# One order of work in a fused state-space and dense kernel: the second dense layer's third product before its second, and one weight load moved

## The chip, the cores and the metric

The kernel runs on one core of a Trainium2 chip. The metric is the device time of one execution in microseconds (us). Before the change it is 587.95 us, the median of 3 runs (587.34 to 588.11). The execution that was profiled took 587.96 us, with a span of 586.7 us between its first and its last instruction. TensorE's granted clock is 1.0 throughout.

## The reference

```python
def _A_ref(x, ...):                       # S5: a diagonal complex state space
    Lam_bar = jnp.exp(dt * Lam)
    B_bar = ((Lam_bar - 1.0) / Lam)[:, None] * Bmat
    Bu = jnp.einsum("bld,pd->blp", x + 0j, B_bar)
    for t in range(L):
        h = Lam_bar[None, :] * h + Bu[:, t, :]
    y = 2.0 * jnp.einsum("blp,dp->bld", hseq, Cmat).real + x * Dskip

def _B_ref(x, w1, b1, w2):                # two dense layers with Mish between
    h = jnp.einsum("bsd,df->bsf", x, w1) + b1
    sp = jnp.log1p(jnp.exp(-jnp.abs(h))) + jnp.where(h > 0, h, 0)
    return jnp.einsum("bsf,fd->bsd", h * jnp.tanh(sp), w2)

xn = _layernorm(x)
out = x + _A_ref(xn, ...) + _B_ref(xn, B_w1, B_b1, B_w2)
```

There are 2048 tokens of width 1024, the state has 1024 complex entries, and the dense layers are 1024 to 3584 to 1024 wide. All inputs are bfloat16.

## The kernel before

**Blocks.** The tokens are worked off in four blocks of 512. A block has dense 1 (28 tiles of 128 hidden columns, with Mish), the state space's projection in, its scans and its projection out, and dense 2, all of which TensorE feeds into eight banks of PSUM. The third block, and the fourth, compute dense 1, the projection in and dense 2 by a scheme of the Strassen kind: the two operands are halved in both dimensions, and seven products of halves stand in for eight. Products 1, 2 and 4 multiply raw halves of the activations, products 5, 6, 7 and 3 sums of them; on the side of the weights products 1, 2 and 3 use raw halves, the others sums.

**Dense 2 of the third block.** Twenty of the 28 activation tiles take part in the seven products, ten in either half (`NFG[2]` is 5, so there are five units of two tiles in each product); the other eight (`PLAIN`) are multiplied in the usual way. A product has two halves i, for two tiles of 128 tokens, each with its own bank and ten matmuls. Product 1 writes banks 0 and 2, product 2 banks 4 and 6, product 7 banks 1 and 3, product 5 banks 5 and 7.

**The ring.** Weights reach TensorE through `ring`, seven slots of 512 KB in SBUF. `items` is the list of everything that goes through it, in order; item number n goes into slot n modulo 7. In the third block an item is a pair of units of 256 KB: `ws` are two units of w1, `tp` two units of w2 as the kernel has prepared them (raw or sums) in the DRAM tensor `w2d`; unit 7p+g belongs to the p-th product of `KIND = (1, 7, 2, 5, 6, 3, 4)` and the group g. So units 0 to 4 are product 1's, 7 to 11 product 7's, 14 to 18 product 2's, 21 to 25 product 5's. `w2` items are raw tiles for the plain part, `c` items the projection out. The loads are issued by SyncE's queue (SP), one after the other (`ring_load`, L481 for `tp`, L486 for `ws`), and each waits until TensorE has done with what was in the slot's half, and for a `tp` unit until its store to `w2d` has landed. Both units of a pair count on one semaphore, and a reader waits for both. Items are released in their order only: `release` moves on while the next item in the list has been used up, and `ring_fill` then issues up to seven items from there.

**The stores.** POOL's queue stores the units to `w2d` (`d2_store`, L1269): the raw ones (products 1, 2, 3) of a group when `d2_row` has scaled it, the sums (5, 7, 6, 4) as VectorE makes them in `d2_sums` (L1297), one at each `k0` of the order. The first three of either kind share a semaphore, which counts only when all three have landed.

**The order by hand.** The instructions of the third block follow a string, `STEPS`; each engine works off its own instructions in that order. The tokens that matter here:

| token | what | engine |
|---|---|---|
| x1 ... y4, z7, z4 | a product of dense 1 for the quads x, y, z of four tiles: 8 matmuls (L1063) | TensorE |
| ez4, ey4, ... | its evacuation (L1083, L1086, L1100) | ACT, VectorE |
| D11, D10 | product 1 of dense 2, halves 1 and 0: 10 matmuls each (L1544); D20, D21, D70, D71 likewise for products 2 and 7 | TensorE |
| X5, X6, X3, X4 | a whole product, 20 matmuls | TensorE |
| g2, g6, g7 | Mish of tiles 12-19, 20-23, 24-27 (L931) | ACT |
| G7 ... G13 | scaling of two tiles each, Gn of tiles 2n and 2n+1 (L938) | ACT |
| t0, t1, t2, ta0 | the sums of activations for products 7, 5, 6 and 3 (L1399) | VectorE |
| E3; lr0, li0; ns, tr | the next block's layer norm | VectorE; ACT, VectorE; ACT, SP |
| r3 to r7; sc, to, so; al | rotations, scans, rotations back; scaling | VectorE; ACT |
| kp2, kp3; kp0, kp1 | product 1's (kp2), 6's (kp3), 7's (kp0), 5's (kp1) banks set aside in `KS` (L1624; L1618) | ACT; VectorE |
| pl24, pl10, pl12, pl26 | two plain tiles each, into all eight banks: 16 matmuls | TensorE |
| Y, Q, fin | the projection out, its end, the addition to x (L1679) | TensorE, TensorE, VectorE |

Product 2 reads tiles 14 to 23 of the activations (their second halves of tokens), the ones that G7 to G11 scale; its matmuls take them in that order, two from each G. t1 reads both the tiles 0 to 9 and 14 to 23 and stands behind G10. Every reader and writer of a buffer waits as program order has it: an instruction that overwrites a tile waits for the earlier ones that read it. A matmul's reading is told by the next matmul of TensorE that signals, which for these halves is the last of the ten.

The pair lists are made at the end of the part that builds `items` (L441 and on): `W_ITEMS[blk]` is the list of w1 pairs in the order of their use in `STEPS` or `LAST`; for the third block it has 19 items, the last of which is the single unit of z4. `SPLIT` is the third and the fourth block, `NB - 1` the fourth.

Of the kernel before, what the change touches and what calls it, by code (L numbers as in the profile page):

```python
# [142 lines left out]
def bass_parallel_sum__ssm_conv_s5__dense_activation_mish__prompt_kernel(  # L143
    nc: bass.Bass,
    A_x: bass.AP,
    A_Lambda_re: bass.AP,
    A_Lambda_im: bass.AP,
    A_B_re: bass.AP,
    A_B_im: bass.AP,
    A_C_re: bass.AP,  # L150
    A_C_im: bass.AP,
    A_log_dt: bass.AP,
    A_Dskip: bass.AP,
    B_x: bass.AP,
    B_w1: bass.AP,
    B_b1: bass.AP,
    B_w2: bass.AP,
    out: bass.AP,
):
    build_kernel(nc, A_x, A_Lambda_re, A_Lambda_im, A_B_re, A_B_im, A_C_re, A_C_im,  # L160
                 A_log_dt, A_Dskip, B_w1, B_b1, B_w2, out)


def build_kernel(nc, A_x, A_Lambda_re, A_Lambda_im, A_B_re, A_B_im, A_C_re, A_C_im,
# [10 lines left out]
    NF = F // P  # L175
# [5 lines left out]
    FAST = 1  # L181
    NPL = 12
    SPLIT = range(2, NB)
    GROUPS = ((0, 7), (7, NPL), (NPL, NPL + 8), (NPL + 8, NF), (12, 16), (16, 20), (20, 24), (24, 28))
    TILES = [*range(12)]
    NFG = {2: 5, 3: GF}
    W2_ORDER = (*range(10), 12, 10, 11, 13)
    EARLY, LATE = ((0, 20),), ((20, 28),)
    PLAIN = [(f, f + 1) for f in (24, 10, 12, 26)]
# [41 lines left out]
    REAL = (3, 2, 0, 1, 4, 5, 6)  # L231
# [4 lines left out]
    def fetched(blk, order, made):  # L236
        us = [(group(blk, QUADS.index(o[0])), int(o[1])) for o in order.split() if o[0] in QUADS and len(o) == 2 and o[1].isdigit()]
        us = [u for u in us if u not in made]
        return [("ws", tuple(us[i:i + 2])) for i in range(0, len(us), 2)]

    ON_CHIP = {FAST: [(5, n) for n in (5, 6, 3, 7)], SPLIT[0]: [(g, n) for g in (2, 0, 1) for n in (5, 6, 3, 7)], NB - 1: []}
    W_ITEMS = {SPLIT[0]: fetched(SPLIT[0], STEPS, ON_CHIP[SPLIT[0]]), NB - 1: fetched(NB - 1, LAST, ())}
    O_ITEMS = [("w1", f // 2) for f in TILES[::2]] + fetched(FAST, WHOLE, ON_CHIP[FAST])
# [155 lines left out]
    def early(name, shape, dtype, where):  # L399
        b_early.append(Buf(name))  # L400
        return nc.alloc_sbuf_tensor_at(name, shape, dtype, offset=base_c + where), b_early[-1]
# [9 lines left out]
    ncs, _ = early("ncs", [P, NR], f32, 10752)  # L411
# [29 lines left out]
    NT = 7 * (NF // 2)  # L441
    items, item_blk = [], []
    for blk in range(NB):
        items += W_ITEMS[blk] if blk in SPLIT else O_ITEMS if blk == FAST else [("w1", g) for g in range(NF // 2)]
        if blk == NB - 1:
            items += [("ts", m) for m in range((NT + 3) // 4)]
        elif blk in SPLIT:
            units = [[7 * p + i for p in ps_ for i in range(NFG[blk])] for ps_ in (range(5), range(5, 7))]
            parts = [[("tp", tuple(us[i:i + 2])) for i in range(0, len(us), 2)] for us in units]
            items += parts[0] + [("w2", (4 * REAL[f // 4] + f % 4) // 2) for f, _ in PLAIN] + parts[1]  # L450
        else:
            items += [("w2", g) for g in W2_ORDER]
        items += [("c", j) for j in range(NJ)] if blk >= FAST else []
        item_blk += [blk] * (len(items) - len(item_blk))
# [1420 lines left out]
```

## Time and profile before

| what | value |
|---|---|
| median of 3 runs | 587.95 us (587.34 to 588.11) |
| profiled execution | 587.96 us |
| its span | 586.7 us |
| TensorE busy | 581.6 us, 99% |
| VectorE busy | 512.3 us, 87% |
| ACT busy | 401.9 us, 68% |
| POOL busy | 151.8 us, 26% |
| dense 2 of the third block, products 1 to plain | 371.7 to some 419.5 us from the span's start |

PE stands for TensorE's matmuls, PEld for its weight loads, DVE for VectorE, SP for SyncE's queue. A timeline row gives the start, the time to the end, the engine, the line of the kernel, the operation, the tiles written and read, the count, and in brackets the idle time before it and what ended that. Matmuls overlap: one of 512 columns lasts 0.38 us in the records though the next one starts earlier. A row of the view by stretches gives the stretch, its length, TensorE's busy time with the count of matmuls, the granted clock, the share of the DMA engines and GB/s.

### The profile page before, as it was taken

To read this page: it belongs to the slowest core of one execution; us is meant where nothing else is said; L and a number is where in the kernel's file an instruction comes from. 1 tells how busy PE (TensorE), PEld (TensorE's weight loads), DVE (VectorE), ACT (ScalarE), POOL (GpSimd) and SP (SyncE) were. 2 spreads that over 40 slices of the span, in tenths; PEclk is the share of its full clock that TensorE was granted. 3 is DMA by queue.
4 is the path that set the end of the run, shared out by engine and by line. 5 is a ranking of instruction groups with operands and counts; after the bars stand their busy time and mean duration, and the time that the engine had idled before them with its cause. 6 is when DMAs were issued, how large, how long until landed. Compare 5 with 4: busy or idle time off the path is not lost.

```text
span 586.7 us, 9766 instructions
## 1 busy us (share of the span) xinstructions
PE 581.6 (99%) x3631; PEld 351.4 (60%) x3631; DVE 512.3 (87%) x784; ACT 401.9 (68%) x541; POOL 151.8 (26%) x215
## 2 busy tenths in 40 slices
PE   8999999999999999999999999999999999999998
PEld 7644444444447887444448888644446888844444
DVE  6999989997997878999877789999997569789995
ACT  4869995558578868999916779976223788992330
POOL 2899300123525420441251243200000013100000
PEclk9999999999999999999999999999999999999999
DMA  9999997999588987899999959998846946989832
GB/s 254 284 254 303 221 188 186 290 320 351 184 287 287 345 281 283 308 320 262 345 372 360 344 205 307 331 361 240 291 158 207 382 165 235 329 326 315 297 113 73
DMA packets 115369, 160.84 MB, mean 274 GB/s; under 512 B 55802, under 2 KB 66682, under 8 KB 115322
## 3 DMA queue, kind: packets, MB, share of 16 engines
q1 hardware_dynamic: 98512, 107.31, 59.6%
q0 software_dynamic: 13728, 45.62, 21.9%
q10 hardware_dynamic: 3082, 7.29, 3.7%
q8 instruction: 29, 0.48, 0.3%
q14 instruction: 18, 0.15, 0.1%
HBM read 114.05 MB, written 34.08 MB: 252 GB/s over the span
## 4 chain that ended last, share of the span: by engine, by line
PE 96%; DMA 2%; SPq 1%; issue 0%; DVE 0%
PE ps L1544 49%; PE ps L1063 19%; PE ps L985 13%; PE ps L1755 10%; PE ps L1773 5%; DMA ring<-in_B_w_dram 1%; PE ps L722 1%; DMA ring<-w2d 1%; PE ps L713 0%; SPq L428 0%; SPq L481 0%; PE ps L547 0%; SPq L489 0%; SPq L432 0%; DVE xx L1709 0%
## 5 line engine op out<-in xcount | busy, mean ns | idle before, releaser
L1544 PE MATMUL ps<-ring,act 128*128 128x512 bf16 (+1 forms) x716 | 156.5, 379 | 0.2 <-DMA ring<-w2d 0.2
L1544 PEld LDWEIGHTS ps<-ring,act 128*128 128x128 bf16 (+1 forms) x716 | 69.7, 98 | 84.1 <-DMA ring<-w2d 1.0
L1083 ACT ACTIVATE snaps<-ps,par,cs 128x256 f32<-128x256 f32 x100 | 54.5, 562 | 42.6 <-PE ps L1063 40.4
L1544 PE MATMUL ps<-ring,hT 128*128 128x512 bf16 (+1 forms) x390 | 83.4, 376 | 0.0
L947 DVE TENSOR_TENSOR mt<-hT,tab 128x2048 bf16<-128x2048 bf16 (+1 forms) x56 | 68.0, 1215 | 0.4
L1544 PEld LDWEIGHTS ps<-ring,hT 128*128 128x128 bf16 x390 | 38.1, 98 | 45.0
L1406 DVE TENSOR_TENSOR_SCAN hT<-cs,qi,hT 128x512 bf16<-128x512 f32 x48 | 60.2, 1275 | 0.0
L1063 PE MATMUL ps<-TT,ring 128*128 128x256 f16 x480 | 59.8, 273 | 0.0
L1755 PE MATMUL ps<-xnT,ring 128*128 128x512 bf16 x264 | 57.3, 379 | 0.0
L1100 DVE SCALAR_TENSOR_TENSOR act<-ps,cs,snaps 128x512 bf16<-128x512 f32 x54 | 39.4, 747 | 16.7 <-PE ps L1063 14.7
L1063 PEld LDWEIGHTS ps<-TT,ring 128*128 128x128 f16 (+1 forms) x480 | 46.8, 98 | 6.5
L1063 PE MATMUL ps<-xnT,ring 128*128 128x256 bf16 x400 | 50.4, 273 | 0.0
L1269 POOL DMA_DIRECT2D w2d<-hb x35 | 25.0, 716 | 87.6 <-ACT hb L1279 50.6
L1755 PEld LDWEIGHTS ps<-xnT,ring 128*128 128x128 bf16 x264 | 25.8, 98 | 31.0
L1650 ACT ACTIVATE hT<-hT,wz 128x1024 bf16<-128x1024 bf16 x16 | 18.0, 1146 | 36.9 <-DVE hT L1646 36.9
L1063 PEld LDWEIGHTS ps<-xnT,ring 128*128 128x128 bf16 (+1 forms) x400 | 39.0, 98 | 5.2
L931 ACT ACTIVATE act<-act 128x2048 bf16<-128x2048 bf16 (+3 forms) x13 | 33.0, 2559 | 2.0 <-DVE act L1086 1.9
L1010 DVE TENSOR_TENSOR hT<-ps,snaps 128x512 f16<-128x512 f32 x36 | 23.8, 687 | 10.3 <-ACT snaps L1002 8.4
L938 ACT ACTIVATE act<-act,cs 128x512 bf16<-128x512 bf16 x48 | 30.8, 709 | 0.1
L1212 POOL DMA_DIRECT2D wsd<-hb x35 | 19.0, 546 | 43.8 <-DVE hb L1238 33.5
L1766 ACT ACTIVATE act<-ps,par 128x512 bf16<-128x512 f32 (+1 forms) x40 | 23.5, 661 | 7.4 <-PE ps L1755 7.4
L1773 PE MATMUL ps<-xnT,BT 128*128 128x512 bf16 x128 | 27.8, 379 | 0.0
(237 smaller groups left out, 1028.1 us busy)
## 6 DMA issues: line engine op xcount, KB each, us to landing
ring<-wsd SPq DMA_DIRECT2D x110, 256.0 KB, 4.6
ring<-in_B_w_dram SPq DMA_DIRECT2D x52, 512.0 KB, 5.4
ring<-ctd SPq DMA_DIRECT2D x24, 512.0 KB, 4.5
ring<-w2d SPq DMA_DIRECT2D x24, 512.0 KB, 4.7
ring<-w2d SPq DMA_DIRECT2D x36, 256.0 KB, 4.4
wsd<-hb POOLq DMA_DIRECT2D x35, 256.0 KB, 5.0
w2d<-hb POOLq DMA_DIRECT2D x35, 256.0 KB, 4.9
hb<-in_B_w_dram POOLq DMA_DIRECT2D x20, 256.0 KB, 5.2
```

The lines of the kernel that those rows point to most:

```text
L931: aop(lambda e: e.activation(t, t, AF.Mish), reads=b, writes=b)
L938: aop(lambda e, a=a, y=y: e.activation(a, a, AF.Copy, scale=y), reads=[b_a, b_y], writes=[b_a])
L947: vop(lambda e: e.tensor_tensor(mt[:], u.unsqueeze(1).to_broadcast([P, 2, 2, TB]), tab[:, :, j, :].unsqueeze(2).to_broadcast([P, 2, 2, TB] ...
L985: PE.mm(lambda e, w=w, x=x, o=o, begin=begin, end=end: e.matmul(ps[:, bank, o:o + TH], lhsT=w, rhs=x, start=opens and begin, stop=end, ski ...
L1063: PE.mm(lambda e, w=w, x=x, o=o, begin=begin, end=end: e.matmul(ps[:, bank, o:o + TH], lhsT=w, rhs=x, start=opens and begin, stop=end, ski ...
L1083: aop(lambda e, o=o, p=p, j=j: e.activation(o, p, AF.Identity, scale=ig, bias=b1(f0 + j)), reads=[b_ps[b], b_par, b_ig], writes=b_dst)
L1100: vop(lambda e: e.scalar_tensor_tensor(out=dst, in0=bank(b), scalar=ig, in1=src, op0=ALU.mult, op1=ALU.add), reads=[b_ps[b], b_snap[k], b_ ...
L1269: PO.dma(lambda e: e.dma_start(w2d[at // 4][:, at % 4 * TB:(at % 4 + 2) * TB].rearrange("p (j t) -> p j t", j=2), t[:, :, d, :]), sem, rea ...
L1406: vop(lambda e: e.tensor_tensor_scan(out=hT[:, ci, j, :], data0=cj("r", j).to_broadcast([P, TB]), data1=hT[:, ci, j, :], initial=init, op0 ...
L1544: PE.mm(lambda e: e.matmul(ps[:, bank, lo:hi], lhsT=lhsT, rhs=rhs, start=opens, stop=last, skip_group_check=split), reads=reads, writes=[b ...
L1755: PE.mm(lambda e, k=k, w=w: e.matmul(ps[:, bank, :], lhsT=w, rhs=xnT[:, k, :], start=k == 0, stop=k == NK - 1), reads=[b_ring[s]] + b_xnT, ...
L1773: PE.mm(lambda e, ci=ci, k=k: e.matmul(ps[:, bank + ci, :], lhsT=BT[:, ci, j, k, :], rhs=xnT[:, k, :], start=k == 0, stop=k == NK - 1), re ...
```

## The change

In the order of the third block the two halves of product 2 (D20, D21) change places with those of product 7 (D70, D71), D20 standing where D70 stood; D70 follows D21, and D71 stands behind g7 and G12. kp0, which reads the banks of product 7, goes behind r5. In the list of ring items the w1 pairs of either of the last two blocks are put down without the last one; in the third block that one, z4's, follows the first two pairs of product 1's units, and the units are listed product 1, 2, 7, 5, 6 in place of 1, 7, 2, 5, 6, so the pairs are (0,1), (2,3), (4,14), (15,16), (17,18), (7,8), (9,10), (11,21) where they were (0,1), (2,3), (4,7), (8,9), (10,11), (14,15), (16,17), (18,21). In the fourth block the last one is put down where it was.

```diff
--- before.py
+++ after.py
@@ -212,7 +212,7 @@
              "ew3 w7 h4 ew7 a2 ea1 b6 eb6 w4 ew4 a5 b3 ea5 a6 eb3 h5 b7 ea6 S0 a3 k0 eb7 a7 ea7 m4 ea3 k0 d2 h6 ed2 G1 c2 a4 b4 h7 ea4 eb4 r0 c1 ec1 k0 c5 "
              "ec5 d5 ed5 d1 c6 k0 ed1 ec6 c3 ec3 d6 G0 ed6 G2 d3 c7 r1 ed3 ec7 l0 x1 h16 d7 ed7 x5 E1 ex1 h17 c4 h18 E0 x2 h19 ex2 ec4 k0 y5 d4 ex5 ed4 E2 "
              "x6 ex6 y1 y2 ey1 ey5 k0 ey2 x7 x3 ex7 ex3 y6 r2 x4 ey6 k0 ex4 k0 z1 z5 ez1 G3 ez5 k0 z2 k0 y7 y3 ez2 k0 z6 z3 ez6 ey7 ez3 g2 D11 G7 ey3 y4 "
-             "k0 ey4 z7 ez7 G8 g6 G9 D10 z4 t0 D70 E3 ez4 G10 t1 kp2 t2 r3 r4 D71 D20 lr0 g7 G12 kp0 D21 r5 G4 G5 X5 li0 X6 r6 kp1 G11 kp3 pl24 ns2 pl10 "
+             "k0 ey4 z7 ez7 G8 g6 G9 D10 z4 t0 D20 E3 ez4 G10 t1 kp2 t2 r3 r4 D21 D70 lr0 g7 G12 D71 r5 kp0 G4 G5 X5 li0 X6 r6 kp1 G11 kp3 pl24 ns2 pl10 "
              "ns0 r7 ns1 G6 G13 tr0 ns3 tr1 tr2 tr3 pl12 pl26 sc20 sc00 sc21 sc50 sc01 sc10 to0 sc11 so0 al0 ta0 X3 to1 so1 sc30 al1 to2 sc41 sc31 so2 to3 "
              "sc60 sc40 al2 so3 sc71 to4 X4 so4 sc51 to5 so5 al4 sc70 al3 sc61 al5 to6 so6 jk0 to7 so7 sk0 al7 sk1 sk2 sk3 al6 Y0 sx0 sx1 sx2 sx3 Y1 Y2 Y3 "
              "Y4 Y5 Q0 fin0 Q1 fin1 ax2 ax3 Q2 fin2 Q3 fin3")
@@ -441,13 +441,13 @@
     NT = 7 * (NF // 2)
     items, item_blk = [], []
     for blk in range(NB):
-        items += W_ITEMS[blk] if blk in SPLIT else O_ITEMS if blk == FAST else [("w1", g) for g in range(NF // 2)]
+        items += W_ITEMS[blk][:-1] if blk in SPLIT else O_ITEMS if blk == FAST else [("w1", g) for g in range(NF // 2)]
         if blk == NB - 1:
-            items += [("ts", m) for m in range((NT + 3) // 4)]
+            items += W_ITEMS[blk][-1:] + [("ts", m) for m in range((NT + 3) // 4)]
         elif blk in SPLIT:
-            units = [[7 * p + i for p in ps_ for i in range(NFG[blk])] for ps_ in (range(5), range(5, 7))]
+            units = [[7 * p + i for p in ps_ for i in range(NFG[blk])] for ps_ in ((0, 2, 1, 3, 4), (5, 6))]
             parts = [[("tp", tuple(us[i:i + 2])) for i in range(0, len(us), 2)] for us in units]
-            items += parts[0] + [("w2", (4 * REAL[f // 4] + f % 4) // 2) for f, _ in PLAIN] + parts[1]
+            items += parts[0][:2] + W_ITEMS[blk][-1:] + parts[0][2:] + [("w2", (4 * REAL[f // 4] + f % 4) // 2) for f, _ in PLAIN] + parts[1]
         else:
             items += [("w2", g) for g in W2_ORDER]
         items += [("c", j) for j in range(NJ)] if blk >= FAST else []
```

## Prediction

> **What bounds the kernel now.** I read the page first: busy times, then the chain of waits.
>
> ```profile
> span 586.7 us, 9766 instructions
> PE 581.6 (99%) x3631; PEld 351.4 (60%) x3631; DVE 512.3 (87%) x784; ACT 401.9 (68%) x541; POOL 151.8 (26%) x215
> PE 96%; DMA 2%; SPq 1%; issue 0%; DVE 0%
> ```
>
> TensorE sets the time. So the change can win only what TensorE loses by waiting, and it loses anything that it makes TensorE wait for. I therefore read the timeline of TensorE through dense 2 of the third block, then the busy time of its dense 2 matmuls over three stretches, then the weight loads in the same place.
>
> ```profile
> 371.70 2.32 PE L1544 MATMUL ps<-ring,act 128*128 128x512 bf16 x10
> 375.60 2.32 PE L1544 MATMUL ps<-ring,act 128*128 128x512 bf16 x10
> 377.76 1.04 PE L1063 MATMUL ps<-TT,ring 128*128 128x256 f16 x8
> 378.63 1.46 PE L1544 MATMUL ps<-ring,S 128*128 128x512 f16 x6
> 380.57 3.20 PE L1544 MATMUL ps<-ring,S 128*128 128x512 f16 x14 [0.47 <-DMA ring<-w2d]
> 383.60 2.07 PE L1544 MATMUL ps<-ring,act 128*128 128x512 bf16 x8
> 385.85 33.84 PE L1544 MATMUL ps<-ring,act 128*128 128x512 bf16 x156 [0.18 <-DMA ring<-w2d]
> ```
>
> ```profile
> 371.70:373.85 2.15, 2.15 (x10) 1.00 1.05 418
> 378.63:385.85 7.22, 6.54 (x28) 1.00 0.93 295
> 385.85:397.08 11.23, 11.23 (x52) 1.00 1.03 376
> ```
>
> ```profile
> 380.56 2.71 PEld L1544 LDWEIGHTS ps<-ring,S 128*128 128x128 f16 x14 [0.97 <-DMA ring<-w2d]
> 384.62 0.56 PEld L1544 LDWEIGHTS ps<-ring,act 128*128 128x128 bf16 x4 [0.49 <-issue]
> 385.85 1.19 PEld L1544 LDWEIGHTS ps<-ring,act 128*128 128x128 bf16 x7 [0.67 <-DMA ring<-w2d]
> ```
>
> The reader is to see the pace: ten unhindered matmuls take 2.15 us, 52 take 11.23, so 0.216 us each. The first product's halves stand at 371.70 and 375.60, the last w1 product (z4) at 377.76, product 7 (on the sums, tile S) from 378.63, product 2 (raw) from 383.60. The 28 matmuls between 378.63 and 385.85 take 7.22 us and need 28 x 0.216 = 6.04. So **this stage loses 1.18 us**, in three places: the weight loads that were held until 380.56, 384.62 and 385.85. The two idle times that the timeline names (0.47 and 0.18) are less than that because its matmul lasts 0.38 us against a pace of 0.216. 1.18 us is 0.20% of the time, and it is all that this change can win.
>
> What they waited for stands in the queue of ring loads (SP): its waits between 364 and 390 us, and its issues.
>
> ```profile
> SPq L481 <- DMA w2d<-hb: 5.2, 2, 3.2
> 368.44 0.32 SPq L481 DMA_DIRECT2D ring<-w2d  x1
> 376.20 1.85 SPq L481 DMA_DIRECT2D ring<-w2d  x2
> 378.87 0.32 SPq L481 DMA_DIRECT2D ring<-w2d  x1
> 379.24 0.43 SPq L481 DMA_DIRECT2D ring<-w2d  x1
> 379.73 0.90 SPq L481 DMA_DIRECT2D ring<-w2d  x2
> ```
>
> ```profile
> DMA to landing us min/median/max: 3.7/5.4/6.3
> DMA to landing us min/median/max: 4.9/4.9/4.9
> 359.12 1.44 POOL L1269 DMA_DIRECT2D w2d<-hb  x2 [1.36 <-ACT hb L1279]
> w2d<-hb POOLq DMA_DIRECT2D x35, 256.0 KB, 4.9
> ```
>
> (The first landing row is for the 15 loads issued from 376 to 385 us, the second for the one at 368.44.) Twice, for 5.2 us together, SP stood before a load of sums whose store to DRAM had not landed, with everything behind it. The later of these is unit 11, issued at 376.20; it and unit 10 share a slot and a count, and product 7 needs unit 10 at its seventh matmul: the 0.64 us lost before 380.57. The other two losses are slots. In the old order z4's item precedes all tp items, and slots come free in order of items, so the slots that product 1 has emptied are refilled only after z4: (16,17) at 378.87 and 379.24, (18,21) from 379.73. Product 2 finds them late, by 0.19 and 0.34 us.
>
> **The change part by part.**
>
> *Fetch order.* One item is moved, no load is added or taken away. z4's item goes behind (0,1) and (2,3): z4 is issued some 3.5 us later than now, when the slot of the item (x4, z1) is free, near 366 (z1 ends six w1 products of 0.87 us, z4's length above, ahead of D11's 371.70), and is needed at 377.76; with the longest landing of the row above, 6.3 us, it is there by 372.3. Cost nothing; cover over 5 us. In exchange (0,1) and (2,3) come one slot earlier, and after D10's fourth matmul (375.60 + 4 x 0.216, and 0.16 for its tail, 376.6) their slots can be refilled at once, not only after z4.
>
> *Order of the units.* (4,14), (15,16), (17,18) now precede (7,8), (9,10), (11,21). The first three need raw units only, whose last stores were issued at 359.12 and, at 4.9 us each, had landed by 366. So SP no longer waits for stores: (15,16) and (17,18) go out as the items (y7, y3) and (z6, z3) are used, the last four w1 products ahead of D11, from 369 to 372. (7,8) follow y4 and z7, which end at 375.60: issued by 376.1, landed at the longest by 382.4, needed by product 7 at its new place, 383. (9,10) is issued by 377.1, landed by 383.4, needed from 383.8; (11,21) by 378.0 and 384.3, needed from 384.7. **All 1.18 us go**, even with the longest landing.
>
> *Product 2 ahead of product 7.* The 20 + 20 matmuls stay the same. What is new is who they wait for. I read ACT and VectorE (DVE), which make its inputs.
>
> ```profile
> 376.45 1.89 ACT L931 ACTIVATE act<-act 128x2048 bf16<-128x2048 bf16 x1
> 378.25 2.54 ACT L938 ACTIVATE act<-act,cs 128x512 bf16<-128x512 bf16 x4
> 397.07 1.27 ACT L1624 ACTIVATE KS<-ps,wz 128x512 f32<-128x512 f32 x2 [5.26 <-PE ps L1544]
> ```
>
> ```profile
> 380.83 3.02 DVE L1399 TENSOR_TENSOR act<-act 128x2560 f16<-128x2560 bf16 x2 [0.16 <-ACT act L938]
> 393.21 1.40 DVE L1618 SCALAR_TENSOR_TENSOR KS<-ps,wz,xx 128x512 f32<-128x512 f32 x2
> 406.50 1.48 DVE L1399 TENSOR_TENSOR act<-act 128x2560 f16<-128x2560 bf16 x1
> 442.18 1.28 DVE L1679 SCALAR_TENSOR_TENSOR xx<-ps,wz,KS 128x1024 bf16<-128x1024 f32 x1 [0.77 <-PE ps L1544]
> 443.91 1.28 DVE L1679 SCALAR_TENSOR_TENSOR xx<-ps,wz,KS 128x1024 bf16<-128x1024 f32 x1 [0.44 <-PE ps L1544]
> 447.69 2.48 DVE L1679 SCALAR_TENSOR_TENSOR xx<-ps,wz,KS 128x1024 bf16<-128x1024 f32 x2
> 453.47 0.75 DVE L1100 SCALAR_TENSOR_TENSOR act<-ps,cs,snaps 128x512 bf16<-128x512 f32 x1 [1.50 <-PE ps L1063]
> ```
>
> The four scalings from 378.25 are G9 and G10, 0.61 us apart. D20 starts at 378.63 and reads G9's second tile at its sixth matmul, 379.71; that tile is done at 378.25 + 0.61 + 0.71 = 379.57. No wait, by a tenth. G10 is another matter: it stands behind D20 in the order and overwrites tiles that D20 reads, so **ACT gains a wait for D20's end**: 378.63 + 9 x 0.216 + 0.38 = 380.95, with the 0.04 that kp3's row shows from a product's end to its start 381.0. G10 then ends at 382.32, not 380.80. D21 starts at 380.79 and its eighth matmul, due at 382.30, reads G10's second tile: it can go at 382.36. A weight load that must wait may cost its own 0.10 us on top; then it is 0.16. In this trace the held load and its matmul both stand at 385.85, so I take 0.06, and 0.10 with the wobble of D20's sixth. The bounds are 0 and 0.3 (both of G10's instructions end to end, 0.71 each, and the load).
>
> The Trainium skill (TensorE: Matmul & The Clock Gate, "Architectural detail") says that a matmul may begin before its weight load has completed. By that rule the price is 0.06, without it 0.16; the equal start times at 385.85 bear it out, and the forecast moves by 0.1 us between the two.
>
> Behind G10 on ACT are kp2, the root, g7, G12, G4, G5, G11, all 1.5 us later; ACT then stood idle for 5.26 us before kp3, which hides it. Behind G10 on VectorE is t1: it starts at 382.35 and not at 380.83, and **everything on VectorE comes 1.52 us later**, while TensorE comes 1.1 us earlier. VectorE has no pause from there to 442.18, so I check each meeting. kp1 (393.21) ends near 396.1; pl24 reads its banks from 396.8: free. kp0, now behind r5 and D71, is still ahead of kp1 on VectorE: free. ta0 (406.50) ends at 406.50 + 1.48 + 1.52 = 409.50. The product that needs it, X3:
>
> ```profile
> 410.68 0.59 PE L1544 MATMUL ps<-ring,act 128*128 128x512 bf16 x2
> 450.65 1.91 PE L1063 MATMUL ps<-TT,ring 128*128 128x256 f16 x16
> ```
>
> X3 starts after 64 plain matmuls, 397.08 + 13.80 = 410.88 (the row's second), and would come at 409.78; its weight load 0.2 sooner, 409.57. Margin 0.07 us: free, but barely. At the block's end the pauses before fin0 (442.18) and fin1 (443.91), 0.77 and 0.44 us, absorb most of the delay and leave 0.31. q5 of the fourth block (450.65) would come at 449.57 and needs fin2, which ends at 447.69 + 1.28 + 0.31 = 449.28: free, by 0.2 to 0.3. The pause of 1.50 us before 453.47 takes up the rest.
>
> **Sum**, against the profiled execution of 587.96 (span 586.7): -1.18 + 0.10 = -1.08, that is 586.88. It agrees with the median of the runs, 587.95, to 0.01. Two small costs remain possible at the near margins (X3, and (4,14) below), for which I add 0.05: **586.9 us**.
>
> **The rivals.**
>
> *The wait moves into the first product.* Unit 4 now shares its slot's count with unit 14 and not 7; both second halves are issued at 368.44, and the load took 4.9 us, to 373.34. D11's ninth matmul starts at 371.70 + 8 x 0.216 = 373.43. There is no reserve. (15,16) now follows at once, where SP used to stand still; with the 5.4 of the later median D11 loses 0.4, with 6.0 it loses 1.0. For it: the crowd. Against: fewer loads are in flight ahead of it. Time 587.3 to 587.9; I price it at 587.5.
>
> *It does not do what it says.* If DMA bandwidth and not order is the limit, loads issued earlier land no earlier. For: a DMA share near 1 in the rows above. Against: 418 GB/s in one stretch, 295 in the very stretch that loses. Time 587.95.
>
> *Slower: VectorE falls behind for good.* The place is ta0 before X3. If VectorE's delay is d, X3 waits d - 1.6; the kernel is no faster from d = 2.7. The reason for a larger d: t1 waits for all of G10, and G10 for all of D20. Were VectorE to lose D20's full 2.15 and G10's 1.32, d is 3.5, X3 loses 1.9, and the time is 586.9 + 1.9 = 588.8. Against: VectorE already waited for G10 today, so only the shift of G10, 1.5, should count.
>
> **How the numbers follow.** Forecast 0.64, first rival 0.20, second 0.08, slower 0.08. What this measurement tells from no change is about 0.2%, 1.18 us: below 586.77 is faster, above 589.13 slower. The forecast lies 0.13 short of the first bound, and the runs before spread over 0.77, so a little under half of its chance counts as faster: 0.30. Slower by that much needs the last rival and more: 0.05. The rest, 0.65, is no difference. The range goes from the full 1.18 and 0.3 of spread, 586.4, to halfway into the slower case, 588.2.
>
> **What would show it.** Right: no idle time of TensorE before product 7 and at most 0.16 us inside product 2; 40 matmuls from z4's end in 8.7 to 8.8 us; no SP wait on w2d<-hb there; t1 near 382.4 with ACT named; X3 without a wait. Wrong: a held weight load in D11, a wait on VectorE before X3 or q5, or loads from 376 on that take longer than 6.3 us.

## The result and the profile after

The changed kernel takes 586.99 us (median of 22 runs, 586.19 to 588.6), the kernel before it 588.15 us beside it (22 runs, 587.33 to 589.67). The ratio is 0.9979, with a 95% interval of 0.9973 to 0.9986: about 1.2 us, between 0.8 and 1.6. The forecast was 586.9. The profiled execution took 587.59 us.

From the page of the changed kernel: the span, the busy times and the chain of waits.

```profile
span 586.3 us, 9766 instructions
PE 582.0 (99%) x3631; PEld 353.3 (60%) x3631; DVE 513.7 (88%) x784; ACT 401.8 (69%) x541; POOL 151.8 (26%) x215
PE 98%; DMA 1%; SPq 0%; DVE 0%; issue 0%
```

The span is only 0.4 us shorter than before. Where the rest went is seen in TensorE's timeline through dense 2 of the third block:

```profile
372.33 2.32 PE L1544 MATMUL ps<-ring,act 128*128 128x512 bf16 x10
376.23 2.32 PE L1544 MATMUL ps<-ring,act 128*128 128x512 bf16 x10
378.39 1.04 PE L1063 MATMUL ps<-TT,ring 128*128 128x256 f16 x8
379.26 4.63 PE L1544 MATMUL ps<-ring,act 128*128 128x512 bf16 x20
383.73 4.48 PE L1544 MATMUL ps<-ring,S 128*128 128x512 f16 x20
388.05 3.19 PE L1544 MATMUL ps<-ring,act 128*128 128x512 f16 x14
446.75 1.04 PE L1063 MATMUL ps<-xnT,ring 128*128 128x256 bf16 x8
```

The first product starts at 372.33, 0.63 us later than in the trace before (371.70). The order ahead of this place is the same in both kernels, so the difference comes from earlier in the execution: 13 us after the span's start TensorE already stands 0.42 us later than in the trace before. The reader is therefore to count from the first product's start. Products 2 and 7 now stand as two rows of 20 with no idle time in brackets. The last row is the fourth block's first dense 1 product, 74.42 us after the start of the first product; before, it stood at 447.16, 75.46 us after:

```profile
447.16 1.04 PE L1063 MATMUL ps<-xnT,ring 128*128 128x256 bf16 x8
```

So **the change is worth 1.04 us** in this trace, and all of it arises inside the stage: from the first product's start to that of the first plain product (pl24) it is 25.39 us before and 24.35 after, and nothing is given back until the fourth block. At the full pace of 0.216 us the stage would take 24.20; 0.15 is still lost. The weight loads of the changed kernel show where:

```profile
380.26 2.35 PEld L1544 LDWEIGHTS ps<-ring,act 128*128 128x128 bf16 x12 [0.24 <-ACT act L938]
383.07 0.33 PEld L1544 LDWEIGHTS ps<-ring,act 128*128 128x128 bf16 x3 [0.47 <-ACT act L938]
410.37 1.52 PEld L1544 LDWEIGHTS ps<-ring,act 128*128 128x128 f16 x8 [0.21 <-DVE act L1399]
```

The first is D20's sixth, held by G9 but ahead of its matmul's turn, so TensorE lost nothing. The second is D21's eighth, held by G10: the matmul due at 382.93 (0.216 after the one at 382.72) came at 383.07, which is 0.14 us. The third is X3's first, held by ta0, again without a loss. ACT and VectorE, in the timeline of either:

```profile
381.68 1.33 ACT L938 ACTIVATE act<-act,cs 128x512 bf16<-128x512 bf16 x2 [1.48 <-PE ps L1544]
```

```profile
383.05 3.02 DVE L1399 TENSOR_TENSOR act<-act 128x2560 f16<-128x2560 bf16 x2 [1.75 <-ACT act L938]
408.83 1.48 DVE L1399 TENSOR_TENSOR act<-act 128x2560 f16<-128x2560 bf16 x1
```

G10 has gained its wait for D20, and t1 a wait of 1.75 us for G10. ta0 ends at 410.31; X3's load stands at 410.37.

The queue of ring loads: its waits from 364 to 390 us, the loads issued from 369 to 374, and the stores to `w2d` issued from 355 to 380, in the changed kernel.

```profile
SPq L481 <- DMA w2d<-hb: 0.2, 1, 0.2
```

```profile
L481 SPq DMA_DIRECT2D ring<-w2d x5: 319/320/1347, 369.0 to 372.5; - x5
DMA to landing us min/median/max: 4.7/6.2/7.0
```

```profile
L1269 POOL DMA_DIRECT2D w2d<-hb x11: 707/719/732, 357.7 to 375.7; - x11
DMA to landing us min/median/max: 3.2/5.4/7.2
```

SP's 5.2 us of waits for stores have become 0.2. But loads and stores have grown longer in the stretch where the loads now crowd: up to 7.0 us from issue to landing, where the forecast took 6.3 for the longest, and the stores up to 7.2. The load of 7.0 us is the last of the five, issued at 372.52, the second half of (17,18). It landed at 379.53, 1.03 us ahead of the matmul that needs it, D20's seventh (379.26 + 6 x 0.216 = 380.56). The stores' row of the kernel before:

```profile
DMA to landing us min/median/max: 3.0/4.7/5.2
```

### The profile page after: what moved, and what is told of

Its sections match the earlier page's. It is cut to its first block, busy times and chain, and to the rows that moved or that the text cites. A ratio compares the mean times of both kernels' runs of the same rounds, so it can differ in the third digit from the quotient of the medians.

```text
span 586.3 us, 9766 instructions
## 1 busy us (share of the span) xinstructions
PE 582.0 (99%) x3631; PEld 353.3 (60%) x3631; DVE 513.7 (88%) x784; ACT 401.8 (69%) x541; POOL 151.8 (26%) x215
## 4 chain that ended last, share of the span: by engine, by line
PE 98%; DMA 1%; SPq 0%; DVE 0%; issue 0%
PE ps L1544 50%; PE ps L1063 19%; PE ps L985 13%; PE ps L1755 10%; PE ps L1773 5%; PE ps L713 1%; PE ps L722 1%; DMA ring<-in_B_w_dram 1%; PE ps L547 0%; SPq L432 0%; PE ps L582 0%; DVE xx L1709 0%; SPq L428 0%; PE ps L750 0%
```

## The experiments

Stage times are from the start of the first product to that of pl24, as above. In the traces of the experiments the records of a few matmuls are missing, always the same ones (the first of D11 and of pl24 among them, so that D11's row shows nine); there the start is taken one pace, 0.216 us, ahead of the second. The medians of the experiments are of 6 to 11 runs, the ratios on record are to the kernel before on the same chip, whose medians beside them were 588.10 to 588.58 us. Each stage time is that of one trace.

| kernel | stage, us | median, us | ratio (95%) |
|---|---|---|---|
| before | 25.39 | 588.15 | |
| the change | 24.35 | 586.99 | 0.9979 (0.9973 to 0.9986) |
| without z4's move | 25.38 | 587.93 | 0.9996 (0.9982 to 1.001) |
| z4's move alone | 25.32 | 588.17 | 0.9998 (0.9989 to 1.0007) |
| G10 ahead of product 2 | 24.93 | 587.51 | 0.9985 (0.9977 to 0.9994) |
| product 2 split around G10 | 24.37 | 586.98 | 0.9974 (0.9963 to 0.9984) |
| 1.6 us more on VectorE ahead of ta0 | 24.70 | 588.66 | 0.9995 (0.9981 to 1.0009) |
| the same in the kernel before | 25.36 | 588.14 | 0.9995 (0.9986 to 1.0004) |
| r3 ahead of t1 | 24.35 | 587.3 | 0.998 (0.9972 to 0.9989) |
| r3 ahead of t1, and 1.6 us more ahead of ta0 | 24.35 | 586.8 | 0.9973 (0.9961 to 0.9984) |
| split, and z4 behind three pairs | 24.20 | 586.67 | 0.9971 (0.9958 to 0.9984) |
| the change, once more | 24.35 | 587.53 | 0.9976 (0.9967 to 0.9985) |

The medians hardly separate neighbours in this table; the stages do.

### Are both parts of the change needed?

First the change with z4's item back ahead of all units:

```diff
-        items += W_ITEMS[blk][:-1] if blk in SPLIT else ...
+        items += W_ITEMS[blk] if blk in SPLIT else ...
-            items += parts[0][:2] + W_ITEMS[blk][-1:] + parts[0][2:] + ...
+            items += parts[0] + ...
```

> The changed kernel with z4's item back ahead of all tp items; the order of the products and of the units as changed. Stage means here D11's first matmul to X6's last, 112 + 24 matmuls of dense 2 and w1: 25.38 us before, 24.35 after, 24.2 at full pace. My theory (slots come free in the order of items, so what product 1 empties waits for z4): (9,10) is issued only after z4, like (16,17) before at 378.9 and 379.2, lands near 384.5 and holds D70's fifth matmul by 0.5 to 0.6 us; (11,21) holds its ninth by 0.3 to 0.5. With the 0.14 inside D21 the stage is 25.2 to 25.4, and the time within 0.2 us of before. Rival (it is the stores: raw units first is all that counts): stage 24.4, time 1.0 to 1.2 us below before.

The stage took 25.38 us, the median is 0.9996 of before. SP's waits for stores are gone there. TensorE's timeline:

```profile
383.05 1.89 PE L1544 MATMUL ps<-ring,S 128*128 128x512 f16 x8
385.80 2.76 PE L1544 MATMUL ps<-ring,S 128*128 128x512 f16 x12 [0.86 <-DMA ring<-w2d]
```

One loss of 1.02 us stands at D70's ninth matmul (385.80 against 383.05 + 8 x 0.216), which reads unit 11. The slots that product 1 has emptied are again refilled only after z4, and now the late unit is the last of the new order. The stage is as long as expected, but by one late pair and not by two: (9,10) went out at 378.84, when z4 had ended (377.71 + 1.04), and landed by 383.35, ahead of D70's fifth matmul at 383.92. Only (11,21), landed at 385.75, held TensorE.

Then z4's move alone, the units and products as before:

```diff
-        items += W_ITEMS[blk] if blk in SPLIT else ...
+        items += W_ITEMS[blk][:-1] if blk in SPLIT else ...
-            items += parts[0] + ...
+            items += parts[0][:2] + W_ITEMS[blk][-1:] + parts[0][2:] + ...
```

> The kernel before with z4's item behind the first two pairs and nothing else changed; products in the old order 1, 7, 2. My theory: the wait for unit 11's store stays, so D70's seventh matmul still loses 0.64 us; (16,17) and (18,21) go out some 0.4 us earlier than before, and of their 0.53 us 0 to 0.25 remain. Stage 24.9 to 25.1, time 0.3 to 0.5 us below before. Rival (SP's place in the queue is all that counts): all three losses go, stage 24.2, time 1.2 below.

This missed: 25.32, and no gain (0.9998). Its timeline, SP's waits, and the load of unit 11:

```profile
378.91 1.46 PE L1544 MATMUL ps<-ring,S 128*128 128x512 f16 x6
381.31 3.19 PE L1544 MATMUL ps<-ring,S 128*128 128x512 f16 x14 [0.94 <-DMA ring<-w2d]
384.56 13.76 PE L1544 MATMUL ps<-ring,act 128*128 128x512 bf16 x62
```

```profile
SPq L481 <- DMA w2d<-hb: 5.2, 2, 2.9
```

```profile
L481 SPq DMA_DIRECT2D ring<-w2d x1: 320/320/320, 376.4 to 376.4; - x1
DMA to landing us min/median/max: 4.9/4.9/4.9
```

The two slot losses are gone, as expected: product 2 follows from 384.56 without a bracket. But the wait for the pair (10,11) grew from 0.64 to 1.10 us (381.31 against 378.91 + 6 x 0.216). The load of unit 11, issued at 376.4, took 4.9 us to land. In the kernel before it went out at 376.20 and took 4.3:

```profile
L481 SPq DMA_DIRECT2D ring<-w2d x1: 320/320/320, 376.2 to 376.2; - x1
DMA to landing us min/median/max: 4.3/4.3/4.3
```

What differs behind it is that the next loads follow at once, where z4's slot had held them back. That they slow the one ahead fits, but no run here isolates it. What is shown is that the three losses cannot be priced one by one: **each half of the change alone is worth nothing (0.01 and 0.07 us of the stage), both together 1.04**.

### The price of G10's new place

G10 is put ahead of D20, where it need not wait for it. Both halves of product 2 then read tiles 20 and 21 as G10 leaves them, as in the kernel before. (In the changed order D20 stands ahead of G10 and takes these two tiles as Mish left them, while D21 takes them scaled; tiles 22 and 23 stand ahead of their scaling, G11, in every kernel here. So the change is not one of order alone: it also changes what D20 multiplies. The runs here tell its time only.)

```diff
-... D10 z4 t0 D20 E3 ez4 G10 t1 kp2 t2 r3 r4 D21 D70 ...
+... D10 z4 t0 G10 D20 E3 ez4 t1 kp2 t2 r3 r4 D21 D70 ...
```

> The changed kernel with G10 ahead of D20, so that D20 takes tiles 20 and 21 as G10 has scaled them (in the changed kernel D20 takes them as Mish left them). My theory: D20's seventh and eighth matmuls now wait for G10's two instructions, 0.31 and 0.39 us; D21 loses its 0.14 no longer; t1 is back at 0.1 us behind ez4. Stage 24.9, time 0.6 us above the changed kernel, 0.4 to 0.5 below before. Rival (ACT's wait for D20 is the dearer way round, through VectorE): time at or below the changed kernel's.

Measured 24.93. TensorE and VectorE:

```profile
378.31 1.46 PE L1544 MATMUL ps<-ring,act 128*128 128x512 bf16 x6
380.53 2.98 PE L1544 MATMUL ps<-ring,act 128*128 128x512 bf16 x13 [0.76 <-ACT act L938]
```

```profile
380.51 3.02 DVE L1399 TENSOR_TENSOR act<-act 128x2560 f16<-128x2560 bf16 x2 [0.16 <-ACT act L938]
```

D20 now stops for G10, 0.7 us in the stage, and t1 waits only 0.16 us for it. (The second half of (17,18) took 8.4 us here and landed 0.37 us after D20's seventh matmul was due. The stop for G10's second tile, done at 380.48, hides that.) So the place behind D20 is the cheaper one for TensorE by 0.58 us, and VectorE pays for it.

Both prices can be avoided by working off six matmuls of either half first, and the four on tiles 20 to 23 after G10's scaling:

```diff
-... z4 t0 D20 E3 ez4 G10 t1 kp2 t2 r3 r4 D21 D70 ...
+... z4 t0 D20.0.6 D21.0.6 E3 ez4 G10 t1 kp2 t2 r3 r4 D20.6.10 D21.6.10 D70 ...
```

> The changed kernel with product 2 as D20 rows 0 to 5, D21 rows 0 to 5, then (behind G10) D20 rows 6 to 9, D21 rows 6 to 9: both halves read tiles 20 and 21 scaled, and by the time TensorE comes to them, 2.59 us after product 2 begins, G10 is done. My theory: no wait left, stage 24.2, t1 back at 0.1 us behind ez4, X3's weight load no longer held; time 1.2 us below before, 0.1 to 0.2 below the changed kernel. Rival (changing banks twelve rows earlier or SP's later release of slots costs something): stage above 24.35.

Products 2 and 7 lost nothing, and t1 followed without a wait. But the stage took 24.37 us, for a wait that the changed kernel's trace does not have. TensorE, its weight loads, and VectorE:

```profile
378.96 4.48 PE L1544 MATMUL ps<-ring,act 128*128 128x512 bf16 x19
383.27 4.48 PE L1544 MATMUL ps<-ring,S 128*128 128x512 f16 x20
```

```profile
373.73 0.11 PEld L1544 LDWEIGHTS ps<-ring,act 128*128 128x128 bf16 x2 [0.49 <-DMA ring<-w2d]
```

```profile
380.99 3.02 DVE L1399 TENSOR_TENSOR act<-act 128x2560 f16<-128x2560 bf16 x2
```

The load at 373.73 is D11's ninth, which reads unit 4. The pair (4,14) landed then: its second half went out at 368.5 and took 5.1 us, and D11 lost 0.16. This is the prediction's first rival. The list of items and the order up to this place are the changed kernel's, so the wait is one of this execution and not of the split.

### Is (4,14) without reserve?

In the split kernel, z4's item goes behind three pairs in place of two, so that (4,14) takes the slot that z4 had:

```diff
-            items += parts[0][:2] + W_ITEMS[blk][-1:] + parts[0][2:] + ...
+            items += parts[0][:3] + W_ITEMS[blk][-1:] + parts[0][3:] + ...
```

> The kernel with product 2 split around G10 (its halves' first six matmuls, then the scaling's four), and z4's item behind the first three pairs of w2 units in place of two. (4,14) then takes the slot that z4's unit took and goes out near 366.5 us, one slot earlier than at 368.2 and 369.0; z4's goes out near 368.2 and, with the longest landing seen, 7.0 us, is there by 375.2, needed at 378. Theory (the 0.16 us at the first product's ninth matmul comes from (4,14), which had no reserve): no weight load of D11 waits, the stage from D11's first matmul to pl24's first is 24.2 us (full pace) against 24.37, nothing else changes; the median 586.8 to 587.0, 0.9970 to 0.9980 of before. Rival (the crowd of loads around 366 to 372 is what is late, whichever unit it is): the wait stays in D11 or moves to D10 or to z4, and the stage is 24.37 or more.

```profile
371.48 2.10 PE L1544 MATMUL ps<-ring,act 128*128 128x512 bf16 x9
378.20 4.48 PE L1544 MATMUL ps<-ring,act 128*128 128x512 bf16 x19
382.52 4.48 PE L1544 MATMUL ps<-ring,S 128*128 128x512 f16 x20
445.54 1.04 PE L1063 MATMUL ps<-xnT,ring 128*128 128x256 bf16 x8
```

```profile
L481 SPq DMA_DIRECT2D ring<-w2d x1: 320/320/320, 366.2 to 366.2; - x1
DMA to landing us min/median/max: 5.3/5.3/5.3
```

(The last fence is the second half of (4,14).) In it the first fence's row of nine has lost its first record, so D11 began at 371.48 - 0.216 = 371.27. The load landed at 371.5, 1.5 us ahead of D11's ninth matmul, due at 371.27 + 8 x 0.216 = 373.0. The stage took 24.20 us, the full pace, and the fourth block starts 74.28 us after the first product began: **all of the 1.18 us is won**. The theory held in this trace: with a reserve of 1.5 us (4,14) did not come late, and nothing else did. This is the fastest version, 0.9971 of before; from the changed kernel, 0.9976 beside it, the ratios do not separate it.

> The changed kernel itself, beside the one above on the same chip. Theory: 0.9979 of before again (0.997 to 0.9987), stage 24.35 us with 0.14 us lost at D21's eighth matmul; the kernel above is 0.0 to 0.3 us faster, which the medians hardly separate. Rival: (4,14) also comes late in some executions of the changed kernel, so that the stage is longer than 24.4 us here.

The changed kernel took 24.35 us in the stage again, with the same 0.14 lost, and no wait in D11. Seven traces of this document have the changed kernel's list of items and its order up to D11 (the changed kernel twice, G10 ahead of product 2, the split, and three of the sections below); the rival's wait stands in one of them, the split's. The second half of (4,14) landed 0.16 to 0.9 us ahead of D11's ninth matmul in the other six: in the changed kernel's first trace it went out at 369.03 and landed at 373.70, and the matmul was due at 374.06. That there is no wait in one trace of the kernel above therefore proves little by itself; it is the reserve of 1.5 us that does.

### The margin of VectorE

A second layer-norm statistics step (E3, which writes what the first wrote) is put ahead of ta0: 1.42 + 0.21 us of VectorE, no other engine. Once in the changed kernel, once in the kernel before:

```diff
-... so0 al0 ta0 X3 ...
+... so0 al0 E3 ta0 X3 ...
```

> The changed kernel with the statistics E3 computed a second time right ahead of ta0: 1.6 us more on VectorE (two of 0.69 and one of 0.21, with their 0.03 between), same values, nothing else. My theory (the change has used up VectorE's margin; X3's weight load already stood 0.2 us for ta0, under cover of the matmul before it, and 0.12 us is left): X3 waits 1.4 to 1.5 us for ta0, and the time rises by 1.4 us, to 0.2 to 0.3 above the kernel before. Rival (VectorE lies off the path, as its 88% and the chain of waits say): no wait before X3, time as the changed kernel.

> The kernel before with the same second E3 ahead of ta0. My theory: ta0 ended at 407.98 there, X3 began at 410.88, so a margin of 2.7 us; 1.6 more cost nothing, time within 0.1 us of before. Rival (that much on VectorE costs either kernel, by the block's end): 0.5 to 1.5 us above before.

TensorE in the changed kernel with the step:

```profile
371.50 2.10 PE L1544 MATMUL ps<-ring,act 128*128 128x512 bf16 x9
...
382.69 1.89 PE L1544 MATMUL ps<-ring,S 128*128 128x512 f16 x8
384.76 2.76 PE L1544 MATMUL ps<-ring,S 128*128 128x512 f16 x12 [0.18 <-DMA ring<-w2d]
...
410.86 3.41 PE L1544 MATMUL ps<-ring,act 128*128 128x512 bf16 x15 [0.89 <-DVE act L1399]
447.13 1.04 PE L1063 MATMUL ps<-xnT,ring 128*128 128x256 bf16 x8
```

VectorE in the kernel before with the step:

```profile
407.50 1.44 DVE L1399 TENSOR_TENSOR act<-act 128x2560 f16<-128x2560 bf16 x1
```

In the changed kernel X3 waited 0.89 us by the bracket. The fourth block begins 75.84 us after the first product (447.13 less 371.50 and the 0.216 of the missing record), 1.42 later than without the step: nearly the whole of the 1.6 us reached TensorE. TensorE had lost 0.35 of the 1.42 before, in product 7 (below), and lost the other 1.07 ahead of X3. VectorE was not held by the first loss: it came to this place 36.50 us after the first product's start in both traces (408.83 less 372.33; the step at 407.79 less 371.29). So X3 would have started as late without it. In the kernel before it is 75.43 against 75.46, no cost: ta0 ended at 408.94 there, and X3, 64 matmuls after 396.48, was not due until 410.3. So **the change used up a reserve of VectorE**, and one more step of 1.6 us there takes back all that it brought (0.9995 of before; 588.66 us against 587.3 for the version with r3 moved, measured beside it).

The row at 384.76 is another matter, which no theory expected: D70's ninth matmul waited for the pair (11,21), 0.35 us (384.76 against 382.69 + 8 x 0.216). SP's wait for stores and the stores issued from 370 to 377 in this run:

```profile
SPq L481 <- DMA w2d<-hb: 0.7, 1, 0.7
```

```profile
L1269 POOL DMA_DIRECT2D w2d<-hb x3: 707/707/719, 369.8 to 374.6; - x3
DMA to landing us min/median/max: 6.1/6.1/7.8
```

A store that went out at 370.86 took 7.8 us; SP issued the next load, that of unit 11, at 378.72, as that landed. In the changed kernel's own trace the wait was 0.2 us and D70's ninth matmul was not late. The additional step stands behind this place, so up to here the two are the same kernel, in two executions. Counted from the first product, unit 11's load went out 0.63 us later here, and unit 21's, issued next, took 5.6 us and not 4.9; together they used up the 1.0 us by which the pair had been ahead. So **the change is worth 1.04 us only while no transfer comes late**: of the five traces with its order of loads and products up to pl24, four have the stage at 24.35 us and this one at 24.70, which leaves 0.69.

### Giving VectorE its reserve back

r3, a rotation on VectorE that needs nothing of G10, is put ahead of t1, into the pause of 1.75 us; then the same with the step of before.

```diff
-... D20 E3 ez4 G10 t1 kp2 t2 r3 r4 D21 ...
+... D20 E3 ez4 G10 r3 t1 kp2 t2 r4 D21 ...
```

> The changed kernel with VectorE's r3 ahead of t1, where VectorE stands idle for 1.75 us waiting for G10. My theory: r3 (2.05 us) fills that gap, t1 comes 0.3 us later than in the changed kernel and all behind r3 1.75 us earlier; ta0 ends 1.75 us earlier; TensorE does not wait for either, so the time is the changed kernel's, within 0.1 us, with the margin at X3 back near 1.9 us. Rival: some VectorE delay already costs time later, and the time falls by 0.2 us or more.

> r3 ahead of t1 and the second E3 ahead of ta0 together. My theory: the margin of 1.9 us takes the 1.6 us, X3 does not wait, time as the changed kernel's within 0.2 us. Rival (VectorE's extra 1.6 us cost wherever they are): 1.4 us above the changed kernel.

VectorE with r3 ahead of t1 and the additional step:

```profile
380.19 1.21 DVE L947 TENSOR_TENSOR mt<-hT,tab 128x2048 bf16<-128x2048 f16 x1
382.11 3.01 DVE L1399 TENSOR_TENSOR act<-act 128x2560 f16<-128x2560 bf16 x2
407.42 1.44 DVE L1399 TENSOR_TENSOR act<-act 128x2560 f16<-128x2560 bf16 x1
```

No bracket is left ahead of t1: the pause is filled. The additional 1.6 us now cost nothing. The stage and the time to the fourth block are 24.35 and 74.42 us, the changed kernel's own, and the ratio is 0.9973. That it was the pause ahead of t1 that put VectorE behind is so shown from both sides. Without the additional step r3's move is worth nothing (24.35 again).

## Why the prediction was right

**The stage loses 1.18 us.** Right: the version with nothing left waiting has 74.28 us to the fourth block against 75.46, a difference of 1.18.

**z4's move costs nothing.** Right: z4's row (378.39) follows D10's ten matmuls (376.23 + 10 x 0.216) at pace.

**SP never waits for stores; all of the 1.18 us go.** Right in sum, with two of its terms off. The loads of (15,16) and (17,18) went out where they were put, but took up to 7.0 us and not 6.3. That left 1.03 us of cover for (17,18), and in the trace with VectorE's additional step, where the load took 7.8 us, 0.25. And the stores lengthened too, from 5.2 at the longest to 7.2: the forecast took the one landing row of 4.9 us for all of them. So SP did wait, 0.2 us in the changed kernel's first trace, not at all in its second, and 0.7 in another, where it reached TensorE with 0.35 us. That the sum came out is in this part luck of the cover: the forecast had no term for transfers that slow each other down.

**D20's sixth matmul is free by a tenth; D21's eighth loses 0.10.** The first is right: held, not late. The second cost 0.14, inside the bounds of 0 and 0.3. What is more than forecast is G10's start, 0.05 later than assumed: it came 0.09 us after D20's end (379.26 + 9 x 0.216 + 0.38 = 381.59, against 381.68), where kp3's row had given 0.04. The held load at 383.07 and its matmul again bear the same start time in the records, and G10's second tile was done at 383.01, so the load's own 0.10 us was not paid on top. That agrees with the rule of the Trainium skill (TensorE: Matmul & The Clock Gate, "Architectural detail") that a matmul may begin before its weight load has completed.

**All of VectorE 1.52 us later; X3 free by 0.07.** Right: t1 came 1.59 us later counted from D11, and X3's load was held for 0.21 us but its matmul was not late. The experiment with 1.6 us more reached TensorE with 1.42, which puts the margin between 0.1 and 0.2 us.

**The sum of -1.08** compares with -1.04 in the trace. The profiled execution's own time fell by less (587.96 to 587.59), because it was 0.63 us later when the stage began; over the runs the fall is 0.8 to 1.6 us. That the median of 586.99 lies within 0.1 us of the forecast of 586.9 is partly chance: the kernel before stood at 588.15 beside it, 0.2 above the 587.95 from which the forecast started.

**The rivals.** DMA bandwidth as the limit is out. The view by stretches from 376 to 388 us, of the kernel before and then of the changed one (the columns are the stretch, its length, busy time and count of TensorE, of its weight loads, VectorE, ACT, POOL, then clock, DMA share, GB/s):

```profile
376.00:388.00 12.00, 11.32 (x55) 5.04 (x54) 11.60 (x17) 11.91 (x14) 0.00 (x0) 1.00 0.95 318
```

```profile
376.00:388.00 12.00, 12.00 (x62) 5.79 (x61) 10.04 (x14) 10.46 (x13) 0.36 (x1) 1.00 1.01 370
```

370 GB/s move where 318 did, and the version with z4 behind three pairs reaches the full pace with the same transfers. The wait in the first product exists, but at a price of 0.16 in one trace of seven, and not 0.4 to 1.0: the load in question took 4.7 us in the changed kernel and 5.1 in the split one. The slower rival's mechanism is real too, and the point from which it decides lies where the forecast had put it, at a delay of 1.6 us, or up to 0.2 later; the change's own delay of 1.59 did not reach X3's matmul.

## What to carry to other kernels

Losses that stand in one queue are not a list of prices: take one away and the next in line may inherit its time, so an edit must be costed by where the last late load then stands, as here each half alone was worth nothing and both 1.04 us. When a step of an engine that is 88% busy is made to wait, put work that needs nothing of it into the pause, and count the reserve at the next meeting: here 2.7 us of reserve (ta0's end at 407.98 to X3's weight load, due at 410.68) had shrunk to 0.1 to 0.2 without a sign of it in the time. And measure a change of 0.2% between two fixed points of the stage, which agreed to 0.01 us between the changed kernel's two traces, and not by the whole span of one; but take several traces, since one late transfer moved the same stage by 0.35 us.

## What was not expected of the hardware

The first product's start varies by 1.2 us between traces (371.12 to 372.33 us) though the order ahead of it is the same in all of these kernels; that is more than the change brings, and most of it is there 13 us after the span's start. And the time of a transfer of 256 KB from issue to landing is no property of the transfer. In the kernel before, loads took 3.7 to 6.3 us and stores 3.0 to 5.2. In the changed kernel, where five loads go out between 369.0 and 372.5, the longest took 7.0 and 7.2, and in its execution with VectorE's additional step 7.8 and 7.8. Of the loads issued from 6 us before the first product to 14 us after its start, the longest took 7.0 to 8.4 us in the nine traces that have this crowd, and 6.3 to 6.5 in the three without it. The Trainium skill (DMA: Bandwidth & Descriptors, "Latency and other measured facts") gives the access to HBM as 0.2 us on average and 2 us at high load; the growth by 0.7 to 2.6 us in these rows goes the same way, but no run here shows which part of a transfer grew.
